# First out group of a chunk as pairs of half-height matmuls into two PSUM banks, summed by VectorE

## Chip, cores, metric

One core of a Trainium2 chip. The metric is the device time of one execution in microseconds (us).

## The reference, cut

Causal attention with 16 extra "beacon" keys, then a gated feed-forward block over all tokens:

```python
# B, H, S, Nb, D = 8, 8, 576, 16, 64;  d_model 512, d_ff 1536, 4608 tokens
scores = 0.125 * q @ concat(beacon_k, k).T        # masked causally
a = exp(scores - max); a /= a.sum(-1) + 1e-9
x = (a @ concat(beacon_v, v)).reshape(tokens, 512)
out = (gelu(x @ w_gate) * (x @ w_val)) @ w_out    # float32
```

## The kernel before: the parts concerned

The feed-forward block goes in nine chunks of 512 tokens. While the attention of batch b runs, the out matmuls of chunk b-1 are dealt out between its parts, as work for TensorE (PE) while ScalarE (ACT) computes exps. A chunk has four out groups of 12 matmuls (contraction rows in 12 blocks of 128); each group fills one bank, which VectorE (DVE) copies out. There are eight banks: three score buffers of two banks each, shared with the gate tiles (`psum_s`), and two single ones (`psum_t`, `psum_o`).

```python
psum_s = tile_pool(bufs=3)   # [P, 2, 512] f32: scores, gate/value tiles, two-head outputs
psum_t = tile_pool(bufs=1)   # one bank each
psum_o = tile_pool(bufs=1)

def scores(b, *parts):                      # one "score tile"
    s_ps = psum_s.tile([P, 2, 512], FP32)
    ...   # score_mms: for hi in 0, 1: rows 64*hi..64*hi+63 -> bank hi (64*128 matmuls)
    act(exp_ring[...], s_ps[...], ACT.Exp, scale=QK_SCALE)
    if b: masks(...)                        # on GpSimd (POOL)

def out_store(ci, ti, o_ps, c0=0, c1=D_MODEL):
    keep(nc.vector.tensor_copy(o_sb[:, ti, c0:c1], o_ps)); ...

def out_ps(ti):                             # groups alternate between the two single banks
    pool, tag = ((psum_t, "t"), (psum_o, "o"))[ti % 2]
    return pool.tile([P, D_MODEL], FP32, name="o_ps", tag=tag)

# per batch b = 1..7, o(n) = next n out matmuls of chunk b-1:
preload_act_table_set(SET_EXP)          # ACT loads its exp table, 1.28 us
o(3); scores((0,0)); scores((0,2)); scores((0,1))
o(5); [b == 1: transposes]; ahead(2); o(5)   # ahead: issue two loads for a later batch
scores((0,3),(1,3)); scores((1,0)); scores((1,2)); ahead(2)
o(5); av_head(0, 0 -> psum_t); o(1)     # av_head: exps times v for one head
scores((1,1)); scores((2,0)); scores((2,2)); ...
av_head(0, 1 -> psum_t); o(7)
scores((2,1)); scores((2,3),(3,3)); scores((3,0))
av_head(1, 0 -> psum_o); o(5); ...
```

I number the score tiles of a stage in this order: (0,0) is the first, (1,2) the sixth, (2,2) the ninth, (3,0) the twelfth. With three buffers, tile n may start only when the exp of tile n-3 has read its buffer.

The softmax here doesn't subtract the row's maximum and nothing guards it: scores larger than these inputs give would overflow.

Of the kernel before, what the change touches and what calls it, by code (L numbers as in the profile page):

```python
# [7 lines left out]
P = 128  # L8
# [3 lines left out]
D_MODEL = 512  # L12
D_FF = 1536
F_TILES = D_FF // P
# [26 lines left out]
FP32 = mybir.dt.float32  # L41
BF16 = mybir.dt.bfloat16
ACT = mybir.ActivationFunctionType
ALU = mybir.AluOpType
# [5 lines left out]
def kernel(  # L50
# [12 lines left out]
    nc = tc.nc  # L63
    keep = tc.keep_in_program_order
# [8 lines left out]
    opool = ctx.enter_context(tc.tile_pool(name="opool", bufs=2))  # L73
# [11 lines left out]
    wo_sb = const.tile([P, F_TILES, D_MODEL], BF16, name="wo_sb", tag="wo_sb")  # L85
# [62 lines left out]
    def load_qk(b):  # L148
        for load in qk_loads(b):
            load()  # L150

    def load_v(b):
        for load in key_loads(v, beacon_v, v_ring[b % NRING][:, :, :, 0:D], b):
            load()
# [12 lines left out]
    def mm(out_ap, lhsT, rhs, start, stop, **kw):  # L167
        keep(nc.tensor.matmul(out_ap, lhsT, rhs, start=start, stop=stop, **kw))  # L168

    def act(out_ap, in_ap, func, **kw):  # L170
        keep(nc.scalar.activation(out_ap, in_ap, func, **kw))  # L171
# [6 lines left out]
    def tr_part(b, m, w, dst):  # L178
        qk, kb = qk6[b]
        for r in range(6):  # L180
            for hi in range(2):
                tr(
                    dst[64 * hi : 64 * hi + 64, r * 96 : (r + 1) * 96],
                    qk[0:96, w, 2 * m + hi, r * D : (r + 1) * D],
                )
        if w:
            tr(dst[:, S:SK], kb[:, 2 * m : 2 * m + 2, :])

    def transpose_pe(b, m, by_act=False):
        t_ps = psum_s.tile([P, 2, 1024], BF16, name="t_ps", tag="s")  # L190
        for w in range(2):
            tr_part(b, m, w, t_ps[:, w, :])
        out_ap = qkT[:, m, :, NB:SK].rearrange("p w (t r) -> p w t r", r=6)
        in_ap = t_ps[:, 0:2, 0:S].rearrange("p w (r t) -> p w t r", r=6)
        keep(nc.vector.tensor_copy(out_ap[:, 1], in_ap[:, 1]))
        if by_act:
            act(out_ap[:, 0], in_ap[:, 0], ACT.Copy)
        else:
            keep(nc.vector.tensor_copy(out_ap[:, 0], in_ap[:, 0]))
        keep(nc.vector.tensor_copy(qkT[:, m, 1, 0:NB], t_ps[:, 1, S:SK]))  # L200
# [59 lines left out]
    def scores(b, *parts):  # L260
        s_ps = psum_s.tile([P, 2, 512], FP32, name="s_ps", tag="s")
        c0 = 0
        for m, c in parts:
            score_mms(b, m, c, s_ps[:, :, c0 : c0 + CHUNK_W[c]])
            c0 += CHUNK_W[c]
        (m, c), n = parts[0], len(parts)
        o, w = CHUNK_OFF[c], CHUNK_W[c]
        act(
            exp_ring[:, m : m + n, :, o : o + w].rearrange("p g h c -> p h g c"),
            s_ps[:, :, 0 : n * w].rearrange("p h (g c) -> p h g c", g=n),  # L270
            ACT.Exp,
            scale=QK_SCALE,
        )
        if b:
            for m, c in parts:
                masks(b, m, c)
# [87 lines left out]
    def av(b, m):  # L364
        x = psum_s.tile([P, 2, 512], FP32, name="x_ps", tag="s")
        for hi in range(2):
            attend(b, m, hi, x[:, hi, :])
        normalize(b, m, x, 0, 2)

    def av_head(b, m, hi, pool, tag):  # L370
        x = pool.tile([P, 1, 512], FP32, name="x_ps", tag=tag)
        attend(b, m, hi, x[:, 0, :])
        normalize(b, m, x, hi, hi + 1)
# [10 lines left out]
    def turn_dma(b, m):  # L384
        y_sb, y_before = y_of[b * NPAIR + m], y_of.pop((b - 1) * NPAIR + m)
        keep(nc.vector.tensor_copy(y_sb[0:NB, 0, :, :], y_before[KROWS[4] - NB : KROWS[4], 4, :, :]))
        c0 = b * S - NB
        keep(
            nc.sync.dma_start_transpose(
                out=xT_sb[:, m, c0 : c0 + 5 * P].rearrange("p (j n) -> p j n", n=P),  # L390
                in_=y_sb.rearrange("p j e d -> p (j e d)"),
            )
        )
# [3 lines left out]
    def hold(b, m):  # L397
        x = xT_sb[:, m, b * S : (b + 1) * S]
        keep(nc.gpsimd.tensor_copy(hold_sb, x[:, 0 : S : S - 1]))  # L399
# [9 lines left out]
    h_of, o_of = {}, {}  # L409
# [43 lines left out]
    def gate_val(ci, fi, split=False):  # L453
        gv_mms(ci, fi, *range(K_CHUNKS), split=split, last=True)

    def out_mm(ci, ti, fi, o_ps, c0=0, c1=D_MODEL):
        mm(
            o_ps,
            h_of[ci][:, fi, ti * P : (ti + 1) * P],
            wo_sb[:, fi, c0:c1],  # L460
            fi == 0,
            fi == F_TILES - 1,
        )

    def out_store(ci, ti, o_ps, c0=0, c1=D_MODEL):
        o_sb = o_of[ci][0]
        keep(nc.vector.tensor_copy(o_sb[:, ti, c0:c1], o_ps))  # L467
        n0 = ci * CH + ti * P
        stores.append((out[n0 : n0 + P, c0:c1], o_sb[:, ti, c0:c1]))

# [2 lines left out]
    def store(engine):  # L473
        for out_ap, in_ap in stores:
            keep(engine.dma_start(out=out_ap, in_=in_ap))
        stores.clear()

    def out_ps(ti):
        pool, tag = ((psum_t, "t"), (psum_o, "o"))[ti % 2]
        return pool.tile([P, D_MODEL], FP32, name="o_ps", tag=tag)  # L480

    def out_mms(ci, u0, u1):
        for u in range(u0, u1):
            ti, fi = divmod(u, F_TILES)
            if u == 0:
                o_of[ci] = [opool.tile([P, 4, D_MODEL], FP32, name="o_sb", tag="o_sb"), None]
            if fi == 0:
                o_of[ci][1] = out_ps(ti)
            out_mm(ci, ti, fi, o_of[ci][1])
            if fi == F_TILES - 1:  # L490
                out_store(ci, ti, o_of[ci][1])
                if ci >= N_CHUNKS - 2:
                    store(nc.sync)
# [9 lines left out]
            out=eye,  # L503
# [25 lines left out]
    def ahead(n):  # L529
        for load in loads[:n]:  # L530
            load()
        del loads[:n]
# [52 lines left out]
    for b in range(B):  # L585
        u = [0]

        def o(n):
            out_mms(b - 1, u[0], u[0] + n)
            u[0] += n  # L590

        if b:
            keep(nc.scalar.preload_act_table_set(SET_EXP))
            o(3)
            scores(b, (0, 0))
            scores(b, (0, 2))
            scores(b, (0, 1))
            o(5)
            if b == 1:
                transpose_pe(1, 3)  # L600
            ahead(2)
            o(5)
            scores(b, (0, 3), (1, 3))
            scores(b, (1, 0))
            scores(b, (1, 2))
            ahead(2)
            o(5)
            av_head(b, 0, 0, psum_t, "t")
            o(1)
            scores(b, (1, 1))  # L610
            scores(b, (2, 0))
            scores(b, (2, 2))
            ahead(2)
            av_head(b, 0, 1, psum_t, "t")
            turn_dma(b, 0)
            o(7)
            scores(b, (2, 1))
            scores(b, (2, 3), (3, 3))
            scores(b, (3, 0))
            av_head(b, 1, 0, psum_o, "o")  # L620
            o(5)
            av_head(b, 1, 1, psum_o, "o")
            turn_dma(b, 1)
            scores(b, (3, 1))
            scores(b, (3, 2))
            av(b, 2)
            turn_dma(b, 2)
            o(6)
            av(b, 3)
            turn_dma(b, 3)  # L630
            o(11)
            keep(nc.scalar.preload_act_table_set(SET_GELU))
            for kk in range(K_CHUNKS):
                for fi in range(2):
                    gv_mms(b, fi, kk, last=kk == 3)
        for fi in range(F_TILES):
            if fi >= 2:
                gate_val(b, fi, fi == F_TILES - 1 and b < B - 1)
            if b == 0 and fi in (4, 6, 8):
                transpose_wide(1, (fi - 4) // 2)  # L640
            if fi == 0:
                if b and b + 1 < B:
                    hold(b, 3)
                    load_v(b + 1)
                if b and b + 2 < B:
                    load_qk(b + 2)
                if 2 <= b + 1 < B:
                    transpose_dma(b + 1)
                store(nc.sync)
# [4 lines left out]
    for i, (c0, c1) in enumerate(((0, 384), (384, D_MODEL))):  # L654
        o_ps = out_ps(1 - i)[:, 0 : c1 - c0]
        for fi in range(F_TILES):
            out_mm(N_CHUNKS - 1, 3, fi, o_ps, c0, c1)
        out_store(N_CHUNKS - 1, 3, o_ps, c0, c1)
        store(nc.sync)
# [30 lines left out]
```

## Time and profile before

| | before |
|---|---|
| time, median of 3 runs | 365.67 us (365.66 to 365.91) |
| PE busy | 353.9 us, 97% of the span |
| ACT, DVE busy | 193.0 us (53%), 158.9 us (44%) |
| attention stage, b = 2 to 7 | 19.02 us, but 19.30 for b = 6 |

A stage is counted here and below from the start of the chunk's last value group to the start of the first gate matmul after the attention. (The stretches that the prediction shows begin one group, 0.86 us, earlier and so read 19.88.) PE's matmul ends in the profile are modelled, so that a short wait hides below the recorded 379 ns; starts are to be compared. One full-height 512-column matmul follows another after 0.216 us.

### The profile page before, as it was taken

The numbers are of one execution on the slowest core, as the hardware profiler recorded it, in microseconds if no ns is written. First come the engines' busy times: TensorE is split into PE (matmuls) and PEld (weight loads), VectorE is DVE, ScalarE is ACT, GpSimd is POOL, SyncE is SP. The second block draws the span as 40 slices with busy tenths as digits, with TensorE's granted clock in tenths as the row PEclk, the third lists the DMA queues.
The fourth block names the chain that finished last, engine by engine and source line by source line (L and its number), as shares of the span: only waits on it lengthen the run. The fifth ranks groups of instructions, "written<-read, shape, count | busy, mean of one in ns | idle before, by whom it ended". The sixth has DMA issues, their size and how long they took to land.

```text
span 363.9 us, 7576 instructions
## 1 busy us (share of the span) xinstructions
PE 353.9 (97%) x3092; PEld 184.9 (51%) x3134; DVE 158.9 (44%) x314; ACT 193.0 (53%) x252; POOL 161.1 (44%) x288
## 2 busy tenths in 40 slices
PE   7899999999999999999999999999999999999996
PEld 7665446444654455444644464446544554444443
DVE  4547846343443335433534354334444353333332
ACT  3965788237923593349633891369335953321210
POOL 8934397646537552945384555655330530000000
PEclk9999999999999999999999999999999999999999
DMA  8999999899289943999299929991596042000102
GB/s 107 175 203 204 196 123 101 126 157 194 31 126 154 211 42 76 154 216 71 56 148 218 113 40 127 173 192 24 110 136 136 19 64 109 2 0 31 58 34 110
DMA packets 160418, 41.55 MB, mean 114 GB/s; under 512 B 146944, under 2 KB 155904, under 8 KB 160384
## 3 DMA queue, kind: packets, MB, share of 16 engines
q0 software_dynamic: 104848, 19.11, 67.6%
q1 hardware_dynamic: 55536, 21.96, 30.5%
q8 instruction: 24, 0.39, 0.5%
q14 instruction: 10, 0.08, 0.1%
HBM read 38.27 MB, written 9.44 MB: 131 GB/s over the span
## 4 chain that ended last, share of the span: by engine, by line
PE 96%; DVE 1%; issue 1%; ACT 1%; ACTq 0%
PE gv_ps L168 48%; PE o_ps L168 25%; PE x_ps L168 9%; PE s_ps L168 8%; PE v_ps L168 2%; PE g_ps L168 2%; PE t_ps L176 2%; DVE qkT L235 1%; PE w_ps L168 1%; ACT expT L171 1%; PE y_ps L176 0%; ACT qkT L171 0%; DVE o_sb L467 0%; DVE qkT L239 0%; DVE r_sb L354 0%
## 5 line engine op out<-in xcount | busy, mean ns | idle before, releaser
L171 ACT ACTIVATE ge_sb<-gv_ps 128x512 bf16<-128x512 f32 x101 | 59.4, 597 | 142.0 <-PE gv_ps L168 139.7
L448 DVE TENSOR_TENSOR hT_sb<-gv_ps,ge_sb 128x512 bf16<-128x512 f32 x101 | 69.0, 691 | 111.6 <-ACT ge_sb L171 109.2
L168 PE MATMUL gv_ps<-xT_sb,wg_sb 128*128 128x512 bf16 x402 | 111.2, 379 | 0.5
L168 PE MATMUL gv_ps<-xT_sb,wv_sb 128*128 128x512 bf16 x388 | 107.9, 379 | 0.4
L171 ACT ACTIVATE expT<-s_ps 128x992 bf16<-128x992 f32 (+3 forms) x112 | 100.5, 975 | 6.4 <-PE s_ps L168 4.7
L168 PE MATMUL o_ps<-wo_sb,hT_sb 128*128 128x512 bf16 (+2 forms) x420 | 99.9, 373 | 2.0 <-issue 0.9
L320 POOL TENSOR_SCALAR_AFFINE_SELECT expT<-expT 128x256 bf16<-128x256 bf16 (+1 forms) x140 | 52.2, 391 | 50.5 <-ACT expT L171 49.3
L168 PEld LDWEIGHTS <-wv_sb 128*128 128x128 bf16 x432 | 42.3, 98 | 50.6
L168 PEld LDWEIGHTS <-wg_sb 128*128 128x128 bf16 x432 | 42.1, 98 | 49.9
L168 PEld LDWEIGHTS <-hT_sb 128*128 128x128 bf16 x444 | 39.9, 98 | 41.7 <-DVE y_sb L356 1.6
L168 PEld LDWEIGHTS <-expT 128*128 128x128 bf16 (+1 forms) x960 | 33.7, 97 | 9.8 <-DVE y_sb L356 2.7
L467 DVE COPY o_sb<-o_ps 128x512 f32<-128x512 f32 (+2 forms) x37 | 24.9, 672 | 31.2 <-PE o_ps L168 30.2
L168 PE MATMUL x_ps<-v_sb,expT 128*128 128x65 bf16 (+1 forms) x960 | 37.5, 193 | 0.0
L111 POOL DMA_DIRECT2D v_sb<-in_v_dram x40 | 33.7, 861 | 6.4 <-DMA wg_sb<-in_moe_w_gate_dram 2.5
L168 PE MATMUL s_ps<-qkT 64*128 64x80 bf16 (+5 forms) x528 | 33.0, 250 | 2.8 <-DVE qkT L239 1.6
L111 POOL DMA_DIRECT2D k_sb<-in_k_dram x30 | 25.2, 843 | 15.9 <-DMA q_sb<-in_q_dram 9.8
L356 DVE TENSOR_TENSOR y_sb<-x_ps,r_sb 128x320 bf16<-128x320 f32 (+1 forms) x47 | 28.8, 612 | 1.6
L111 POOL DMA_DIRECT2D q_sb<-in_q_dram x30 | 25.3, 875 | 8.8 <-DVE hT_sb L448 3.2
L354 DVE RECIPROCAL r_sb<-x_ps 128x5 f32<-128x5 f32 (+1 forms) x47 | 9.6, 204 | 42.7 <-PE x_ps L168 42.7
L168 PEld LDWEIGHTS <-qkT 64*128 64x128 bf16 x528 | 17.2, 95 | 18.0 <-issue 12.8
L399 POOL COPY hold_sb<-xT_sb 128x2 bf16<-128x2 bf16 x6 | 1.1, 185 | 31.1 <-DMA xT_sb<-y_sb 31.1
L171 ACT ACTIVATE qkT<-t_ps 64x288 bf16<-64x288 bf16 (+1 forms) x13 | 6.5, 501 | 4.9 <-PE t_ps L176 4.4
(56 smaller groups left out, 128.1 us busy)
## 6 DMA issues: line engine op xcount, KB each, us to landing
out_dram<-o_sb SPq DMA_DIRECT2D x35, 256.0 KB, 7.1
v_sb<-in_v_dram POOLq DMA_DIRECT2D x24, 128.0 KB, 9.3
q_sb<-in_q_dram POOLq DMA_DIRECT2D x18, 128.0 KB, 12.0
k_sb<-in_k_dram POOLq DMA_DIRECT2D x18, 128.0 KB, 5.6
wo_sb<-in_moe_w_out_dram POOLq DMA_DIRECT2D x3, 512.0 KB, 14.9
wg_sb<-in_moe_w_gate_dram POOLq DMA_DIRECT2D x2, 512.0 KB, 11.8
wv_sb<-in_moe_w_val_dram POOLq DMA_DIRECT2D x2, 512.0 KB, 13.2
v_sb<-in_v_dram POOLq DMA_DIRECT2D x8, 112.0 KB, 5.6
```

The source lines that it names most:

```text
L111: keep(nc.gpsimd.dma_start(out=out_ap, in_=in_ap))
L168: keep(nc.tensor.matmul(out_ap, lhsT, rhs, start=start, stop=stop, **kw))
L171: keep(nc.scalar.activation(out_ap, in_ap, func, **kw))
L176: keep(nc.tensor.transpose(out_ap, in_ap, ident[0:n, 0:n]))
L235: keep(nc.vector.tensor_copy(out_ap, in_ap))
L320: nc.gpsimd.affine_select(out=d, in_=d, pattern=[[0, 2], [1, n]], compare_op=ALU.is_ge, fill=0.0, base=0, channel_multiplier=-1,)
L354: keep(nc.vector.reciprocal(r, x[:, :, :, D:DV]))
L356: nc.vector.tensor_tensor(out=y_of[i][:, :, h0:h1, :].rearrange("p j b d -> p b j d"), in0=x[:, :, :, 0:D], in1=r.to_broadcast([P, h1 - h0 ...
L399: keep(nc.gpsimd.tensor_copy(hold_sb, x[:, 0 : S : S - 1]))
L448: nc.vector.tensor_tensor(out=h_of[ci][:, fi, :], in0=gv_of.pop((ci, fi))[1], in1=ge_sb, op=ALU.mult)
L467: keep(nc.vector.tensor_copy(o_sb[:, ti, c0:c1], o_ps))
```

## The change

The score matmuls use the array as two row tiles of 64 rows, the out matmuls as one of 128; going from one to the other, called a switch here, costs PE 0.095 us by the trace before (the prediction reads it off). The change gives the first out group of the chunks b = 2 to 7 the scores' layout: each of its 12 matmuls becomes two of 64 rows side by side, each into a bank of its own; DVE copies one bank out and adds the other. The group's 12 pairs are dealt 3 and 9 around the first scores, and the first matmul of the next group moves from ahead of the second scores to behind them.

```diff
-    def out_store(ci, ti, o_ps, c0=0, c1=D_MODEL):
+    def out_store(ci, ti, o_ps, c0=0, c1=D_MODEL, o_half=None):
         o_sb = o_of[ci][0]
-        keep(nc.vector.tensor_copy(o_sb[:, ti, c0:c1], o_ps))
+        o_ap = o_sb[:, ti, c0:c1]
+        if o_half is None:
+            keep(nc.vector.tensor_copy(o_ap, o_ps))
+        else:
+            keep(nc.vector.tensor_copy(o_ap, o_half))
+            keep(nc.vector.tensor_tensor(out=o_ap, in0=o_ps, in1=o_ap, op=ALU.add))
...
+    def out_half_mms(ci, u0, u1):
+        for fi in range(u0, u1):
+            if fi == 0:
+                o_of[ci] = [opool.tile([P, 4, D_MODEL], FP32, ...), (out_ps(0), out_ps(1))]
+            halves = o_of[ci][1]
+            for g in range(2):
+                r = slice(64 * g, 64 * g + 64)
+                mm(halves[g], h_of[ci][r, fi, 0:P], wo_sb[r, fi, :],
+                   fi == 0, fi == F_TILES - 1, skip_group_check=True)
+            if fi == F_TILES - 1:
+                out_store(ci, 0, halves[0], o_half=halves[1])
...
-            o(3)
+            o(3, b > 1)
             scores(b, (0, 0)); scores(b, (0, 2)); scores(b, (0, 1))   # (three lines)
-            o(5)
+            o(5 if b == 1 else 9, b > 1)
             if b == 1:
                 transpose_pe(1, 3)
+                o(5)
             ahead(2)
-            o(5)
             scores(b, (0, 3), (1, 3)); scores(b, (1, 0)); scores(b, (1, 2))
             ahead(2)
-            o(5)
+            o(5 if b == 1 else 6)
             av_head(b, 0, 0, psum_t, "t")
```

More of the change, by code (lines that the diff above doesn't have):

```diff
@@ L480, in out_ps @@
         return pool.tile([P, D_MODEL], FP32, name="o_ps", tag=tag)
+    def out_half_mms(ci, u0, u1):
+        for fi in range(u0, u1):
+            if fi == 0:
+                o_of[ci] = [opool.tile([P, 4, D_MODEL], FP32, name="o_sb", tag="o_sb"), (out_ps(0), out_ps(1))]
+            halves = o_of[ci][1]
+            for g in range(2):
+                r = slice(64 * g, 64 * g + 64)
+                mm(
+                    halves[g],
+                    h_of[ci][r, fi, 0:P],
+                    wo_sb[r, fi, :],
+                    fi == 0,
+                    fi == F_TILES - 1,
+                    skip_group_check=True,
+                )
+            if fi == F_TILES - 1:
+                out_store(ci, 0, halves[0], o_half=halves[1])
     def out_mms(ci, u0, u1):
@@ L586, with o @@
         u = [0]
-        def o(n):
-            out_mms(b - 1, u[0], u[0] + n)
+        def o(n, halves=False):
+            (out_half_mms if halves else out_mms)(b - 1, u[0], u[0] + n)
             u[0] += n
```

## The prediction

> **What bounds the kernel now.** I read the page's busy shares and its chain that ended last, then one attention stage in the PE timeline, then the same stretch on ACT and DVE, then all six such stages side by side. The page first:
>
> ```profile
> PE 353.9 (97%) x3092; PEld 184.9 (51%) x3134; DVE 158.9 (44%) x314; ACT 193.0 (53%) x252; POOL 161.1 (44%) x288
> PE 96%; DVE 1%; issue 1%; ACT 1%; ACTq 0%
> ```
>
> TensorE is busy 97% of the span and carries 96% of the chain, so only what shortens or delays PE's own sequence counts. PE's modelled ends hide its short waits (one 512-column matmul is recorded as 379 ns, but the next starts 216 ns later), so I read start-to-start distances. The change touches chunks whose out groups run between the score matmuls, b = 2 to 7. The PE timeline of b = 3:
>
> ```profile
> 122.80 1.03 PE L168 MATMUL g_ps<-xT_sb,wg_sb 128*128 128x512 bf16 x4
> 123.67 1.03 PE L168 MATMUL v_ps<-xT_sb,wv_sb 128*128 128x512 bf16 x4
> 124.53 0.81 PE L168 MATMUL o_ps<-wo_sb,hT_sb 128*128 128x512 bf16 x3
> 125.27 0.81 PE L168 MATMUL s_ps<-qkT 64*128 64x512 bf16 x14
> 126.24 2.10 PE L168 MATMUL o_ps<-wo_sb,hT_sb 128*128 128x512 bf16 x9 [0.16 <-issue]
> 128.28 0.77 PE L168 MATMUL s_ps<-qkT 64*128 64x128 bf16 x14
> 128.98 1.25 PE L168 MATMUL o_ps<-wo_sb,hT_sb 128*128 128x512 bf16 x5
> 130.07 0.62 PE L168 MATMUL x_ps<-v_sb,expT 128*128 128x65 bf16 x15
> 130.53 0.38 PE L168 MATMUL o_ps<-wo_sb,hT_sb 128*128 128x512 bf16 x1
> 130.84 0.94 PE L168 MATMUL s_ps<-qkT 64*128 64x80 bf16 x14
> ```
>
> The first column is the start in us. Four full-height 512-column matmuls take 123.67 - 122.80 = 0.87, so 0.216 each. Three of them before the scores should take 0.648, yet 124.53 to 125.27 is 0.743 by the records: 0.095 us is lost where a 128*128 matmul is followed by a 64*128 one. (The x9 is ten by the code, one record missing; its weight load at 126.01 shows it.) Going back, the last 80-column score pair starts at 128.848 and the next full matmul at 128.979, 0.128 after the pair's second half, where pairs inside a burst follow at 0.032: again some 0.095. The same 0.312 stands between the tenth out matmul (127.964) and the scores at 128.276.
>
> ACT in the same stretch, and in the stage as a whole:
>
> ```profile
> 124.48 1.28 ACT L593 ACT_TABLE_LOAD   x1
> 125.78 2.75 ACT L171 ACTIVATE expT<-s_ps 128x1024 bf16<-128x1024 f32 x3
> 128.73 5.35 ACT L171 ACTIVATE expT<-s_ps 128x832 bf16<-128x832 f32 x6 [0.21 <-PE s_ps L168]
> ```
>
> The first exp starts right as the table load ends (125.77), and three follow without a gap until 128.53; ACT then idles 0.21 for PE. This is a second chain close to PE: there are three score buffers, so the sixth score tile must wait for the third exp, the ninth for the sixth.
>
> **What the Trainium skill says.** "TensorEngine Tiling (Array Packing)", section Key Properties: changing the tiling mode, not just the tile, drains the TensorE. The trace agrees, at 0.095 us each way. The same page, Gotcha 1: different row tiles write to different PSUM banks and may not use one bank together; hence two banks and a sum. The trace shows the scores in that form. "TensorE: Matmul & The Clock Gate", Part 3, The mechanism: matmuls of different row groups start about 4 ns apart and run concurrently. The trace has 3 to 4 ns, and the pair after a 512-column pair starts 0.216 later (128.469 to 128.685), so a pair of half-height matmuls costs what one full-height matmul does. "PSUM — Partial Sum Buffer", Specifications: a VectorE instruction may take one tensor input from PSUM; so a copy, then an add. The trace before has no such sum of two banks; the nearest is the gate product (one PSUM and one SBUF input), 691 ns.
>
> **The change part by part, per chunk of b = 2 to 7.**
>
> 1. Matmuls: 12 full-height ones become 12 pairs. 12 x 0.216 either way: no cost, if pairs behave as those of the scores.
> 2. Layout switches. Before: out | scores | out | scores | out. After, the first two out stretches have the scores' layout: one switch ahead of the first three pairs instead of after them, none until the second scores are over. Two of four go: 2 x 0.095 = 0.19 per chunk, times 6 = 1.14 us. The first scores start at the same moment as before, since their one switch only moved ahead of the three.
> 3. Order. The second out stretch is 9 pairs instead of 10 matmuls; the tenth (first of the next group) moves behind the second scores, where six follow instead of five. That is no work, but it takes 0.216 us of filler from ahead of an ACT wait.
> 4. VectorE: the one copy (692 ns) becomes a copy and an add of, I estimate from the gate product, 691 ns. In total 6 x 0.69 = 4.1 us on an engine that is 44% busy and idle there from 128.86 to 130.73. Off the path, if banks come free in time (below).
>
> What ACT makes of it, on b = 3's times. The ninth pair starts at 125.883 + 0.034 + 8 x 0.216 = 127.645; second scores start at 127.861, 0.415 earlier than now. Their third tile (the sixth of the stage, after 0.41 of score work: 128.276 to 128.685 now) would be due at about 128.27, but its buffer is freed by the third exp, which ends at 128.525 before and after, as that chain hangs on the table load. With the 0.05 that such a release takes (exp end 131.350 to matmul 131.401), it starts at 128.577: a new wait of 0.31. Then 0.31 to the next full-height matmul (from 131.401 to 131.709 in a like case), so six out matmuls from 128.885 and the first head at 130.19, against 130.07 now: 0.12 late, with the same out matmuls done by that point. Next, the ninth score tile. Now it waits: it is due at 131.068 + 0.213 = 131.281 and starts at 131.401, 0.12 late, held by the sixth exp. After, the fourth to sixth exps start 0.32 earlier (128.41 instead of 128.73, no idle gap), so that wait falls, and PE arrives at 131.281 + 0.122 = 131.403. Sum per chunk: -0.19 (switches) -0.12 (ninth tile) +0.31 (sixth tile) = about 0.00, rounded. From there the stage runs as now.
>
> The VectorE release: the ninth pair's end to the copy's start takes 0.416 (127.749 to 128.165 now), so the copy of the second half runs 128.065 to 128.757, and its bank, which the next group needs, is free at about 128.81, against 128.885 wanted. Hidden, by under 0.1. The add ends at about 129.48 and its bank is wanted at 130.19. Hidden.
>
> So five chunks give nothing. The sixth differs:
>
> ```profile
> 200.56:220.44 19.88, 19.61 (x246) 11.12 (x248) 8.93 (x21) 16.35 (x18) 9.96 (x23) 1.00 0.96 73
> 239.43:259.60 20.17, 19.74 (x247) 11.18 (x249) 8.93 (x21) 16.27 (x18) 9.98 (x23) 1.00 0.89 74
> 278.59:298.47 19.88, 19.61 (x246) 11.12 (x248) 8.93 (x21) 16.36 (x18) 7.50 (x20) 1.00 0.18 27
> ```
>
> These are stretches from the last gate group to the next stage's first one (first figure after the bounds: length, then PE, PEld, DVE, ACT, POOL). All are 19.88 but b = 6, with 20.17: there the fourth exp started at 245.643 instead of 245.36, and the ninth score tile waited 0.32 instead of 0.12. With exps four to six 0.3 earlier that lateness falls into slack, worth up to 0.29 us once, if it comes again at the same place at all. I take 0.17 for it.
>
> Sum: 365.67 - 6 x 0.00 - 0.17 = 365.5 us.
>
> **The rivals.** (a) All of the drain is gained: 365.67 - 1.14 = 364.5. For it: the chain is PE at 96%, and ACT's waits are small on the page. Against it: three buffers and the gapless exps, as worked out. If a wait for ACT is shorter than I think, part of this appears. (b) A wait takes more than the switch gave: the VectorE copy frees the bank only 0.08 before it is wanted; a further semaphore hop of 0.05 to 0.1, or a slower copy, would cost up to 0.1 per chunk, and the sixth tile's wait may be 0.05 to 0.1 longer: 6 x 0.1 = +0.6, so 366.2. (c) Half-height pairs of long accumulations are slower than a full matmul, by their double weight loads. For it, only that no trace of this shape exists; against it, score pairs of 80 columns follow at 0.032 with two loads each. At 10 ns a pair, 72 pairs would cost 0.7, so about 366.3. (d) VectorE becomes the bound: 44% and a gap of 1.87 us after the copy speak against it; nothing for the time.
>
> **Range and chances.** Gain and loss are both bounded by about 1 us. I place the centre at 365.5 and the 8-in-10 range at 364.7 to 366.2, wider downwards as (a) in part is the likeliest miss. Two per cent is 7.3 us, six times all drains together: faster by over 2% 0.01, within 2% 0.98, slower 0.01.
>
> **What would show it.** Right: the out pairs of the first group 0.216 apart; scores directly after them without the 0.095; the second scores some 0.4 earlier, then a wait of about 0.3 inside them released by ACT's third exp; no wait at the ninth tile; the fourth exp without idle time before it; the stage at 19.88 again, and x6 adds of 128x512 on DVE at about 690 ns. Wrong: pairs over 0.216 apart (c), the six out matmuls waiting for the copy beyond 128.9 on b = 3's clock (b), or no wait inside the second scores and stages of about 19.7 (a).

## More of the kernel before

All timed runs here: granted TensorE clock 0.999 to 1.000, but for seven with 0.986 to 0.995, among them two of dummy_half, where it matters (see there).

## The result, and the profile after

The changed kernel takes 365.72 us (median of 6 runs, 365.23 to 366.01), the one before 365.67 (6 runs, 365.61 to 365.91). The ratio is 0.9999, with a 95% interval of 0.9986 to 1.0012: the same. Ratios here are the mean time of one kernel's runs over that of the other's runs of the same rounds, so not quite the ratio of the medians quoted.

The page after, busy shares and the chain:

```profile
PE 353.7 (97%) x3164; PEld 184.8 (51%) x3206; DVE 162.8 (45%) x320; ACT 192.7 (53%) x252; POOL 161.2 (44%) x288
PE 80%; DMA 8%; POOL 6%; ACT 3%; issue 2%; DVE 0%; ACTq 0%; POOLq 0%
```

72 more matmuls and 6 more DVE instructions are there, DVE is busy 3.9 us longer, PE as long as before. The chain now passes through ACT for 3%: it is followed back to the exps at the new waits. The 8% of DMA and the 6% of POOL all lie before 53 us: in the attention of b = 1, whose work the change leaves alone, a head waited some 0.3 us for a mask on POOL, and the chain turns off there into POOL's loads. That stage took 20.11 us, against 19.97 before. after_nocopy (below), which is the same there, took 19.97 and has a chain of PE 93%, ACT 3% without DMA, so the branch is of the execution and not of the change (dummy_full, without pairs, has the same branch, and 20.41 us for that stage). The stages where the change is show it better. The PE timeline of b = 3, whose clock runs 0.198 us behind that of the kernel before:

```profile
124.83 0.82 PE L168 MATMUL o_ps<-wo_sb,hT_sb 64*128 64x512 bf16 x6
125.48 0.80 PE L168 MATMUL s_ps<-qkT 64*128 64x512 bf16 x14
126.11 2.11 PE L168 MATMUL o_ps<-wo_sb,hT_sb 64*128 64x512 bf16 x18
128.06 0.56 PE L168 MATMUL s_ps<-qkT 64*128 64x128 bf16 x10
128.78 0.37 PE L168 MATMUL s_ps<-qkT 64*128 64x384 bf16 x4 [0.16 <-ACT expT L171]
129.08 1.47 PE L168 MATMUL o_ps<-wo_sb,hT_sb 128*128 128x512 bf16 x5
130.39 0.62 PE L168 MATMUL x_ps<-v_sb,expT 128*128 128x65 bf16 x15
```

Three pairs take 125.48 - 124.83 = 0.65 and the scores follow without the gap of 0.095; nine pairs take 128.06 - 126.11 = 1.95, 0.216 each. Then the second scores break off: the sixth tile's four matmuls stand in a row of their own, behind ACT. Their 0.16 of recorded idle time is 0.32 in starts (128.239 to 128.775 where 0.213 would do). ACT and DVE in the same stretch:

```profile
125.97 5.26 ACT L171 ACTIVATE expT<-s_ps 128x1024 bf16<-128x1024 f32 x6
131.65 1.91 ACT L171 ACTIVATE expT<-s_ps 128x992 bf16<-128x992 f32 x2 [0.42 <-PE s_ps L168]
```

```profile
128.26 0.69 DVE L471 COPY o_sb<-o_ps 128x512 f32<-128x512 f32 x1 [2.57 <-PE o_ps L168]
128.99 0.69 DVE L472 TENSOR_TENSOR o_sb<-o_ps,o_sb 128x512 f32<-128x512 f32 x1
```

Six exps now run without a gap where there were three and three: in these 5.3 us ACT is the bound, and the scores that PE reaches earlier only wait for it. The copy ends at 128.953, 0.13 ahead of the first full-height matmul at 129.081. And the stretches in the form of the prediction:

```profile
200.90:220.86 19.96, 19.64 (x259) 11.16 (x260) 9.62 (x22) 16.27 (x18) 9.10 (x22) 1.00 0.84 71
239.85:259.81 19.96, 19.64 (x259) 11.22 (x260) 9.62 (x22) 16.37 (x18) 10.01 (x23) 1.00 0.94 74
```

Each stage is 0.07 longer than before and the one of b = 6 is 0.21 shorter: 5 x 0.074 - 0.208 = +0.16 us. Where the 0.07 comes from shows further down the stage, which the prediction did not follow. PE before and then after:

```profile
133.78 0.79 PE L168 MATMUL s_ps<-qkT 64*128 64x80 bf16 x18
134.50 0.62 PE L168 MATMUL x_ps<-v_sb,expT 128*128 128x65 bf16 x15
```

```profile
132.80 1.24 PE L168 MATMUL o_ps<-wo_sb,hT_sb 128*128 128x512 bf16 x5
133.97 0.87 PE L168 MATMUL s_ps<-qkT 64*128 64x80 bf16 x18
134.78 0.62 PE L168 MATMUL x_ps<-v_sb,expT 128*128 128x65 bf16 x15
```

The ninth exp on ACT, before and then after:

```profile
133.13 0.95 ACT L171 ACTIVATE expT<-s_ps 128x928 bf16<-128x928 f32 x1
```

```profile
133.45 0.95 ACT L171 ACTIVATE expT<-s_ps 128x928 bf16<-128x928 f32 x1
```

From the tenth tile to the next head, 133.971 to 134.776, is 0.805; before it was 133.782 to 134.504, 0.722. In the changed kernel the twelfth tile waits for the ninth exp, which ends at 134.400; its matmul starts at 134.451. On the common clock that exp ends 0.12 later than before (134.080), as exps seven to nine run in one row and the seventh waits for its scores (the 0.42 above).

### The profile page after: what moved, and what is told of

It is laid out like the page before. It is cut to its first block, busy times and chain, and to the rows that moved or that the text cites. A ratio compares the mean times of both kernels' runs of the same rounds, so it can differ in the third digit from the quotient of the medians.

```text
span 364.1 us, 7726 instructions
## 1 busy us (share of the span) xinstructions
PE 353.7 (97%) x3164; PEld 184.8 (51%) x3206; DVE 162.8 (45%) x320; ACT 192.7 (53%) x252; POOL 161.2 (44%) x288
## 4 chain that ended last, share of the span: by engine, by line
PE 80%; DMA 8%; POOL 6%; ACT 3%; issue 2%; DVE 0%; ACTq 0%; POOLq 0%
PE gv_ps L168 42%; PE o_ps L168 21%; PE x_ps L168 8%; PE s_ps L168 6%; DMA wo_sb<-in_moe_w_out_dram 4%; DMA qk<-in_q_dram 4%; ACT expT L171 3%; POOL qk L111 1%; PE g_ps L168 1%; PE v_ps L168 1%; POOL v_sb L111 1%; POOL q_sb L111 1%; POOL wg_sb L111 1%; POOL wv_sb L111 1%; POOL expT L320 1%
## 5 line engine op out<-in xcount | busy, mean ns | idle before, releaser
L168 PE MATMUL o_ps<-wo_sb,hT_sb 128*128 128x512 bf16 (+3 forms) x492 | 101.0, 373 | 1.3
L168 PEld LDWEIGHTS <-hT_sb 128*128 128x128 bf16 (+1 forms) x516 | 39.5, 97 | 42.4 <-issue 4.1
L469 DVE COPY o_sb<-o_ps 128x512 f32<-128x512 f32 (+2 forms) x31 | 20.7, 668 | 15.3 <-PE o_ps L168 14.2
L168 PEld LDWEIGHTS <-qkT 64*128 64x128 bf16 x528 | 18.1, 95 | 17.2 <-issue 8.9
L471 DVE COPY o_sb<-o_ps 128x512 f32<-128x512 f32 x6 | 4.1, 691 | 15.4 <-PE o_ps L168 15.4
```

What stands on the lines that cost most here:

```text
L168: keep(nc.tensor.matmul(out_ap, lhsT, rhs, start=start, stop=stop, **kw))
L469: keep(nc.vector.tensor_copy(o_ap, o_ps))
L471: keep(nc.vector.tensor_copy(o_ap, o_half))
```

## The experiments

Theory A: the two switches are saved, and waits of score tiles for the exps that free their buffers take their place. Theory C: behind those stands a second wait, for the bank that DVE's copy frees. Rival B: the pairs or the add cost what the switches give. Stages of the kernels, in us by start records (chunks that agree given once; the two dummy kernels and before_again, whose stages are those of the kernel before, are left out):

| kernel | stage | time, median | ratio to before |
|---|---|---|---|
| before | 19.02 (b = 6: 19.30) | 365.67 | |
| changed | 19.09 | 365.72 | 0.9999 |
| order_only | 19.09 | 366.00 | 1.0012 (0.9999 to 1.0025) |
| before_short | 18.83 | 364.04 | 0.9963 (0.9950 to 0.9975) |
| after_short | 18.86 | 364.61 | 0.9979 (0.9965 to 0.9992) |
| after_short_nocopy | 18.61 | 362.92 | 0.9926 (0.9914 to 0.9939) |
| after_nocopy | 19.09 | 365.83 | 1.0012 (0.9998 to 1.0025) |
| after_early | 19.01 (b = 7: 19.06) | 365.42 | 1.0006 (0.9993 to 1.0020) |
| before_early | 19.02 (b = 6: 19.30) | 365.69 | 1.0004 (0.9987 to 1.0021) |
| join | 18.79 (b = 4: 19.03) | 364.28 | 0.9960 (0.9948 to 0.9972) |
| join_shift | 18.83 (b = 4: 19.06) | 364.52 | 0.9966 (0.9955 to 0.9978) |

The kernel before was run again in each of the three sets: medians 365.60 (first four experiments below), 365.41 (the next four) and 365.75 (the last four).

**order_only.** The order of the change without its layout.

```diff
             o(3); scores (0,0), (0,2), (0,1)
-            o(5)
+            o(5 if b == 1 else 9)
...
-            o(5)
+            o(5 if b == 1 else 6)      # all full height, as before
```

> The kernel before, with the out matmuls of b = 2 to 7 split 3, 9, 6 as in the changed kernel, but all full height, one bank, one copy. All four layout switches stay. Theory A (what the two saved switches give is taken by the waits of score tiles for the exps that free their buffers): the two switches lie inside the sixth tile's wait for the third exp, so this runs as the changed kernel does: stage 19.95 to 19.97 us in each chunk, second scores with a wait of about 0.11 at the sixth tile, the head 0.12 late, some 0.07 at the twelfth tile; 365.7, ratio to before 1.000 within 0.001. Theory B (the switches are really saved on the path, and something of the pairs or of the add costs it back): without pairs and add and with all switches this runs as the kernel before, stage 19.88, and no new wait.

Measured: 366.00 us, correct, and the same stage as the changed kernel to the nanosecond level (19.093 to 19.094, there 19.092 to 19.094).

```profile
126.50 1.89 PE L168 MATMUL o_ps<-wo_sb,hT_sb 128*128 128x512 bf16 x8 [0.16 <-issue]
128.33 0.89 PE L168 MATMUL s_ps<-qkT 64*128 64x128 bf16 x14
129.15 1.47 PE L168 MATMUL o_ps<-wo_sb,hT_sb 128*128 128x512 bf16 x6
```

This is the PE timeline of b = 3 (one of the nine matmuls is missing from the records). The second scores take 0.89 instead of 0.77: a wait of about 0.12 at the sixth tile. With all four switches and no pairs the stage is as long as with two switches fewer. So in this order the two switches cost nothing, since PE would spend the time waiting for the third exp anyway: its last matmuls start 0.052 after that exp's end (128.844 and 128.792). It refutes B's form in which the add or the pairs eat the gain: neither is here.

**before_short, after_short.** Exps of b = 2 to 7 do half of their columns, so that ACT is out of the way (the result is not meant to be right. The comparison proves nothing: the ring keeps older exps, and by an estimate from the reference's inputs, random with a deviation of 0.1, the scores are of the order of 0.01, so that every exp is close to 1 in any batch).

```diff
         o, w = CHUNK_OFF[c], CHUNK_W[c]
+        we = w if b < 2 else w // 2
         act(
-            exp_ring[:, m : m + n, :, o : o + w]..., s_ps[...],
+            exp_ring[:, m : m + n, :, o : o + we]..., s_ps[...][:, :, :, 0:we],
```

> The kernel before, where each exp of b = 2 to 7 does only the first half of its columns (wrong result on purpose): ACT is taken out of the way. Theory A: the ninth tile's wait of 0.12 us and the late mask before the last head pair (0.09) go, and the one long stage of b = 6 becomes like the others: stage 19.68, so 365.7 - 6 x 0.2 - 0.3 = 364.2. Theory B: ACT is no part of it, 365.7.

> The changed kernel with the same halved exps (wrong result on purpose). Theory A alone: the two switches now show in full, 1.14 us under before_short, 363.0. Theory C (behind the exps stands a second wait: the bank that VectorE's copy of the second half frees, 1.16 us after the last pair's start, while PE then wants it after 0.92): most is taken again, by a wait of about 0.25 at the first full out matmul after the second scores; 0.0 to +0.06 us a chunk against before_short, 364.2 to 364.6. Theory B: 365.7.

Measured: 364.04 and 364.61. The first is as theory A says: stages of 18.83, 0.19 shorter, and b = 6 like the others. The second is C's case: the stage is 18.86, no shorter than before_short's, although no tile waits for an exp. PE and then DVE in b = 3 of after_short:

```profile
127.13 0.76 PE L168 MATMUL s_ps<-qkT 64*128 64x128 bf16 x14
128.08 1.46 PE L168 MATMUL o_ps<-wo_sb,hT_sb 128*128 128x512 bf16 x5 [0.19 <-DVE o_sb L472]
```

```profile
127.34 0.69 DVE L472 COPY o_sb<-o_ps 128x512 f32<-128x512 f32 x1 [2.57 <-PE o_ps L168]
```

The scores are whole again, and the wait has moved to the first full-height matmul: it starts at 128.081, 0.385 after the last score matmul where a switch alone takes 0.128, and 0.05 after the copy's end at 128.028.

**after_short_nocopy.** The same without any reader of the second bank (wrong: relative error 0.24).

```diff
-            keep(nc.vector.tensor_copy(o_ap, o_half))
-            keep(nc.vector.tensor_tensor(out=o_ap, in0=o_ps, in1=o_ap, op=ALU.add))
+            keep(nc.vector.tensor_copy(o_ap, o_ps))
```

> The same with the second half's copy and the add replaced by one copy of the first half (result wrong on that account too), so that nothing has to read the second bank before PE writes it again. Theories A and C: both waits are gone and the two switches show in full: 6 x 0.19 = 1.1 us under before_short, about 363.0. If it stays at before_short, the pairs cost what the switches give (B).

Measured: 362.92 us. With both waits out of the way the stage is 18.61, against 18.83 of before_short: 0.213 per chunk, 1.28 us in six. This is the gain of the two switches, shown in full; B is refuted here a second time, since the pairs are in.

```profile
127.45 0.76 PE L168 MATMUL s_ps<-qkT 64*128 64x128 bf16 x14
128.14 1.47 PE L168 MATMUL o_ps<-wo_sb,hT_sb 128*128 128x512 bf16 x5
```

PE again, b = 3: 0.69 from the second scores to the out matmuls, 0.95 in after_short.

**dummy_full, dummy_half.** The price of a switch, where PE waits for nobody: 48 small matmuls between gate tiles.

```diff
+            if b > 1 and 2 <= fi <= 9:
+                d_ps = psum_o.tile([P, D_MODEL], FP32, name="d_ps", tag="o")
+                mm(d_ps[:, 0:D], idle[0:P, 0:P], idle[0:P, 0:D], True, True)   # half: rows 0:64
```

> Control for the next run: the kernel before with 48 extra full-height matmuls of 64 columns (zeros into a free bank), one after each of eight gate tiles in b = 2 to 7, where PE waits for nobody. No layout switch is added. A 64-column matmul should cost 0.03 us: 48 x 0.03 = 1.4, so 367.1.

> The same 48 matmuls over the first 64 rows only, so that each has the scores' layout between two full-height ones: 96 layout switches more than the control. Theory A and C (a switch costs 0.095 us of PE wherever it stands): 96 x 0.095 = 9.1 us over the control, 376.2. If the drain belonged to something else in the attention stage (operands, waits), it stays at 367.

Measured: 367.22 and 378.17 us; both correct. By the profiled executions' spans, 365.5 and 375.6, the 96 switches cost 10.1 us, 0.105 each; by the medians 10.95, 0.114 each. The second figure is too high: of the four runs of dummy_half two had a lower granted clock, 379.68 us at 0.986 and 379.00 at 0.990, and the two at 0.999 to 1.000 took 377.12 and 377.34. These two lie 10.0 us above the control's median, 0.104 per switch. The timelines of dummy_half, then dummy_full, at one insertion:

```profile
149.37 0.81 PE L168 MATMUL gv_ps<-xT_sb,wv_sb 128*128 128x512 bf16 x3
150.12 0.20 PE L168 MATMUL d_ps<-idle 64*128 64x64 bf16 x1
150.25 0.61 PE L168 MATMUL gv_ps<-xT_sb,wg_sb 128*128 128x512 bf16 x2
```

```profile
150.06 0.19 PE L168 MATMUL d_ps<-idle 128*128 128x64 bf16 x1
150.09 0.81 PE L168 MATMUL gv_ps<-xT_sb,wg_sb 128*128 128x512 bf16 x3
```

The small matmul is followed after 0.03 in the array's own layout and after 0.13 in the other one; another 0.095 lie ahead of it, and the first matmul after a switch is followed 0.227 instead of 0.216 later. So a switch costs PE 0.095 to 0.106 us (with that 0.011) in both places where it was measured, and is no effect of the attention stage.

**after_nocopy.** The changed kernel, exps whole, without the second bank's reader (the same edit as above; wrong, relative error 0.24).

> The changed kernel with the second half's copy and the add replaced by one copy of the first half (wrong result on purpose). Theory A with C behind it: the bank's release lies inside the time that PE loses to the exps (free at about 128.82 on the clock of b = 3 before, wanted at 128.88), so nothing changes: stage 19.957, 365.7. If the bank were what holds the changed kernel, the stage falls by up to 0.25 us and the time by up to 1.5.

Measured: 365.83 us, stage 19.093, unchanged. As the kernel stands, the bank's wait costs nothing: it ends inside the one for ACT. The two waits are not added; the later one decides.

**after_early.** An attempt to get the gain: the exps start earlier. The last two gate tiles are interleaved so that the last gelu, and the table load behind it, come before the value matmuls; the first two score tiles go ahead of the three pairs.

```diff
+            if 0 < b < B - 1 and fi >= F_TILES - 2:
+                if fi == F_TILES - 2:
+                    gate_val_last_two(b)     # gate 10, gate 11, (gelus), value 10, value 11
-            o(3, b > 1)
+            [b == 1: o(3)]
             scores(b, (0, 0))
             scores(b, (0, 2))
+            [b > 1: o(3, True)]
             scores(b, (0, 1))
```

> The changed kernel with the last two gate tiles of chunks 1 to 6 interleaved (both gate parts, then both value parts), so that the gelu and the table load behind it end 0.86 us earlier, and with the first two score tiles ahead of the first three out pairs, which all have one layout: the exps start about 0.67 us earlier. Theory A and C: no wait for an exp at the sixth and twelfth tile, instead the second half's bank is waited for, about 0.25 us at the first full out matmul; stage 19.72 to 19.81, so 0.07 to 0.16 us under the kernel before in each of six chunks: 364.7 to 365.2. If exps alone held the changed kernel (A without C), stage 19.56 and about 363.7.

Measured: 365.42, stage 19.01: a miss, only 0.014 under the kernel before. The wait for the third exp is gone and the bank's one is there, as theory C says (the first full-height matmul is again 0.385 after the last score matmul). What I had counted off besides, the wait at the twelfth tile, stays at 0.08: it hangs on exps seven to nine, which begin only when their own scores do, not on when the stage's first exp started.

**before_again, before_early.** The kernel before once more, and with the interleaving alone.

> The kernel before, unchanged, for one more profile: do all six stages take 19.88 us here, or is the one of b = 6 again 20.17? If the long stage belongs to the kernel, it comes again at b = 6; if it is a chance of one execution, it is elsewhere or missing.

> The kernel before (full height, all four switches) with the last two gate tiles of chunks 1 to 6 interleaved, so that the table load ends 0.86 us earlier. The first exp is then bound by the first scores, 0.07 earlier, and the ninth tile's wait falls from 0.12 to 0.05: from the last value matmul's start to the next chunk's first gate matmul 0.07 us a chunk less, 365.6 - 0.4 = 365.2.

Measured: 365.68 for one execution, and 365.69. The long stage of b = 6 is there in both, 19.301 us, as in the first profile and in both dummies': it belongs to the kernel, at its fourth exp, 0.28 late. In the changed kernel the same exp is late too, by 0.19, but PE does not need it by then. The profile puts the lateness down to a mask on POOL; why in this one batch is open. The interleaving alone gives nothing: the first exp starts 0.011 earlier, not 0.07, as the scores were ready as late as the table.

**join, join_shift.** A version that avoids both waits. With 11 pairs, the twelfth block becomes one full-height matmul after the second scores, added into the first half's bank; so the second half's bank is full one matmul earlier and wanted one later.

```diff
 # on after_early
+    def out_join(ci):
+        fi, o_ps = F_TILES - 1, o_of[ci][1][0]
+        mm(o_ps, h_of[ci][:, fi, 0:P], wo_sb[:, fi, :], False, True, skip_group_check=True)
+        out_store(ci, 0, o_ps, o_half=True)      # the add; the copy is issued after pair 11
-            o(5 if b == 1 else 9, b > 1)
+            o(5 if b == 1 else 8, b > 1)
...
+            if b > 1:
+                out_join(b - 1); u[0] += 1
             o(5 if b == 1 else 6)
 # join_shift besides, for b > 1: o(7) -> o(8) before scores (2,1), o(5) -> o(4) after av_head(1,0)
```

> The changed kernel with that interleaving and the early first scores, and with 11 pairs only: the twelfth row block is one full-height matmul after the second scores, added into the first half's bank. The second half's bank is then complete 0.22 us earlier and wanted 0.22 us later, so its wait (0.25) is gone, and the exps are early enough that the shorter filler meets no wait at the sixth tile. Theory A and C: 0.25 us a chunk under after_early, 365.5 - 6 x 0.25 = 364.0. If the time stays at 365.4, the bank's wait was replaced by one that I don't see.

> The same with one out matmul moved from after the first head of pair 1 to before the tenth score tile, which gives the ninth exp 0.22 us to end before its buffer is wanted by the twelfth tile: that wait of 0.08 goes too, 6 x 0.08 = 0.5 under join, 363.5.

Measured: join 364.28 us, correct, ratio 0.9960 (0.9948 to 0.9972). In join's b = 3, PE and then DVE:

```profile
126.99 0.76 PE L168 MATMUL s_ps<-qkT 64*128 64x128 bf16 x14
127.68 1.71 PE L168 MATMUL o_ps<-wo_sb,hT_sb 128*128 128x512 bf16 x7
```

```profile
127.19 0.69 DVE L524 COPY o_sb<-o_ps 128x512 f32<-128x512 f32 x1 [2.35 <-PE o_ps L168]
128.11 0.69 DVE L493 TENSOR_TENSOR o_sb<-o_ps,o_sb 128x512 f32<-128x512 f32 x1 [0.23 <-PE o_ps L168]
```

No wait in the scores or behind them: the copy ends at 127.88, when the first of the seven full-height matmuls, which needs the other bank, is running. The stage is 18.79, 0.21 under after_early's and 0.23 under before's. It is the fastest kernel of this study that computes everything, by 0.4%, which is under the 2% that count as faster here. One chunk, b = 4, is 0.24 longer: a gate product on DVE was late there and held the third tile's buffer; why is open.

join_shift is a miss: 364.52, expected 363.5. The wait at the twelfth tile is gone (0.723 from the tenth tile to the head), but the filler taken from behind that head lets the next head, into the same bank, wait 0.11 for the normalised product of the first. The stage is 0.04 longer than join's. The two runs' ratios overlap; the stages decide.

## Why the prediction was right

The predicted 365.5 us stands against 365.72; the range held it, and the class is "same". The class was safe from the start, as all drains together were 1.14 us of the 7.3 that make two per cent; what was tested is the mechanism. By its steps:

1. Pairs at no cost: right, 0.216 per pair in the trace.
2. Two switches saved, 0.19 per chunk: right in kind; with both waits away the gain is 0.213, as the first matmul after a switch is also followed 0.011 later. Confirmed apart by the dummies.
3. The sixth tile waits for the third exp: right. Predicted start 128.577, found 128.577 on the common clock (128.775 - 0.198); first full-height matmul 128.885, found 128.883; head 130.19, found 130.189. order_only, with all four switches, has the same stage: this wait swallows what they give.
4. No wait at the ninth tile, PE there at 131.403: found 131.404.
5. VectorE hidden: right. Copy from 128.065, found 128.064; add 691 ns. That it was hidden only behind ACT's wait is shown by after_short against after_nocopy: with the exps out of the way the same copy holds PE, as rival (b) feared.
6. "From there the stage runs as now": wrong. This is the step that was mis-sized. The seventh to ninth exps follow PE's lateness of 0.12, and the twelfth tile then waits 0.08 for the ninth exp: +0.074 per chunk, not 0.00, or 6 x 0.074 = 0.44 us in all.
7. The long stage of b = 6 taken as -0.17: the lateness of 0.28 went wholly, near the "up to 0.29" of the prediction; less the 0.074 of step 6 the stage is 0.208 shorter. It was held for possibly a chance; it came in all five profiles with this order and whole exps (before, before_again, before_early and both dummies).

The sum was 6 x 0.00 - 0.17 = -0.17; the traces give 5 x 0.074 - 0.208 = +0.16, and the medians +0.05. The scatter of the changed kernel's runs, 0.8 us, is larger than either, so the timed runs can't tell these sums apart; the stages do. That the missed 0.44 us left the number inside the range is owed to the range's width of 1.5 us and in part to luck, as step 7 gave back more than was taken for it. Rival (a), all of the drain gained, would have been right had PE been alone on the path; rival (c), slow pairs, is refuted, and of (d) nothing shows: DVE is busy 45%. (Counted from the centre of 365.5, rivals (b) and (c) come to 366.1 and 366.2, 0.1 less than written; nothing hangs on it.)

## What to carry to other kernels

When an engine's work is cut ahead of a wait, ask first what ends that wait: here three score buffers tie PE to ACT's exps, and a fixed gain on PE turned into waiting, until join started the exps earlier and freed the second bank sooner. Take suspected waits away one at a time and then together, since a second wait may stand behind the first and only the later one counts. Removing a layout switch of about 0.1 us pays only where PE would not spend that time waiting anyway.

## What the Trainium skill lacked or had wrong

- "TensorEngine Tiling (Array Packing)", Key Properties, says that a change of tiling mode drains the TensorE but gives no cost. Here it is 0.095 us between starts, each way between 128 and 64 rows, and 0.105 per switch over 96 of them (10.1 us).
- "TensorE: Matmul & The Clock Gate", Back-to-back issue gap, gives about 131 ns per matmul as the sustained rate at N = 512 in a stream of weight loads and matmuls, and says that its figure for an isolated matmul, about 216 ns, is too high there. Here such a stream runs at 216 ns, at a granted clock of 1.000, in full-height matmuls and in pairs alike: the page's 216 holds and its 131 does not.
- No page gives as one figure the release chain that set the second wait here: from the start of an accumulation's last matmul to the start of VectorE's copy 0.416 us, the copy 0.69, and 0.05 until PE writes the bank again, 1.16 in all.
